# A spectral filter beside a gated MLP: the inverse 32-point product with high and low parts stacked on 128 partitions

## The chip, the cores and the metric

The kernel runs on one core of a Trainium2 chip. The metric is the device time of one execution in microseconds, the median over runs. The program is written with a tile framework: it traces instructions in program order, and a planner with its own cost estimates then orders each engine's instructions and sets all semaphores.

## The reference

```python
def reference(A_x, A_w_r, A_w_i, B_x, B_w_gate, B_w_up, B_w_down):
    xn = _layernorm(A_x, axis=-1)                       # x: 1 x 2048 x 576
    X = rfft2(xn, axes=(-2, -1)) * (A_w_r + 1j * A_w_i) # 2048 x 289 complex weights
    A = irfft2(X, s=(2048, 576))
    g, u = xn @ B_w_gate, xn @ B_w_up                   # 576 -> 4608
    return A_x + A + (sigmoid(g) * u) @ B_w_down        # 4608 -> 576
```

All inputs and the output are fp32.

## The kernel before

Two computations share one core. The gated MLP gives most of the matmuls: 36 slices of the 4608 hidden columns, for each of two halves ("pairs") of the 2048 rows. A slice of one half is a *unit*: seven products of seven matmuls of 512 columns (L710, into the PSUM banks `pA`, `pB`, `pE`), with ScalarE copying banks out (L788 to L806) and VectorE combining them (L803, L823, L825). The products of the down projection are matmuls of 288 columns into `ps` (L1060), taken out by VectorE or ScalarE (L994 is one such addition); a unit's seven turns each carry some of those.

The spectral part runs in pieces between the turns of the second half. Matmuls are fp32r, and a factor is split into a high part (what the format keeps) and a low part (the rest). The transform over the 2048 rows is taken as 64 x 32, over the 576 columns as one matrix; there are `NQ` = 290 columns of frequencies.

- `phase1b` (16 calls): the column transform and the 64-point one, which writes high and low parts to DRAM (`sc1`).
- `phase2` (16 calls): the 32-point transform forward, times the weights (`ri`, here `wr` and `wi`), and the 32-point transform back, into DRAM (`sc2`). In the forward product, the contraction of 64 (real and imaginary parts of 32) is doubled to 128 by having the high parts on the first 64 partitions and the low parts on the other 64; two matrices (`bm[:, 0]`, `bm[:, 1]`) give main sum and correction on two halves of the output, and VectorE adds the halves. In the inverse product two places (of the 64) lie on the 128 partitions, with a matrix that doesn't mix them; high and low parts are two tiles `zh`, `zl`, and three matmuls are accumulated for each pair of places: high by high, low by high, high by low.
- `phase3` (16 calls): the 64-point transform back, and the columns, added to the result.

Each phase is a Python generator. A `yield` ends its share of one schedule step; a schedule step is one turn of a unit (one product), and every active generator is taken on by one share in it, oldest first. When the calls begin stands in one line, start and distance in schedule steps; before the first call of a phase, `stage2` or `stage3` frees the room of the phase before and loads the constant matrices:

```python
U1, U2, U3 = (0, 4.1), (76, 4.1), (151, 4.5)
for (base, rate), phase, n in ((U1, phase1b, NT), (U2, phase2, N2 // 2), (U3, phase3, NT)):
    for t in range(n):
        begin.setdefault(1 + base + int(t * rate), []).append(lambda t=t, phase=phase: phase(t))
```

PSUM tiles from `pair(...)` are two banks; all of them, `pb`, `pc`, `py`, `pz`, `pe` of the phases and `ps` of the down products, come from the same two buffers in turn, so a new pair waits until the one before last has been taken out. A tile with `bufs=1` has one buffer: its next user waits for the last reader. Nearly all loads and stores are issued from the one queue of SyncE (SP), in order; a DMA that waits there holds back the ones behind it, among them the next units' weights (`w` from `wsp`, L323) and the down weights (`wf` from `fsp`, L957).

L1100 are the additions that gather the parts of the down products late in the last stage.

Of the kernel before, what the change touches and what calls it, by code (L numbers as in the profile page):

```python
# [9 lines left out]
F32 = mybir.dt.float32  # L10
F32R = mybir.dt.float32r
I32 = mybir.dt.int32
AF = mybir.ActivationFunctionType
OP = mybir.AluOpType
# [29 lines left out]
KR = 3 * REM  # L44


U1, U2, U3 = (0, 4.1), (76, 4.1), (151, 4.5)


KOF = np.array(list(range(1, HD, 2)) + [0] + list(range(0, HD + 1, 2)))  # L50
# [18 lines left out]
def _cplx(m):  # L69

    return np.block([[m.real, m.imag], [-m.imag, m.real]])


def _constants():
    out = {}

    mid = np.arange(HD) - (D - 1) / 2
    ang = 2 * np.pi * mid[:, None] * KOF[None, :] / D
    t = np.zeros((P, 2, 5, NQ), np.float32)
    for e, v in ((0, np.cos(ang)), (1, -np.sin(ang))):  # L80
        m = np.where(FREQ, v - (v.mean(0) if e == 0 else 0), 0.0)
        hi, lo = _split(m)
        for part, w in ((0, hi), (1, lo)):
            t[:, e, 2 * part] = w[:P]
            t[:, e, 2 * part + 1] = w[P:2 * P]
        t[:KR, e, 4] = np.concatenate([hi[2 * P:], hi[2 * P:], lo[2 * P:]])
    out["cf"] = t.reshape(P, 10 * NQ)


    s1 = np.arange(N1)  # L90
    k1 = np.arange(N1)
    am = np.zeros((P, N2, 2, P), np.float32)
    ai = np.zeros((P, N2, 2, P), np.float32)
    for s2 in range(N2):
        ph = 2 * np.pi * (((N2 * s1[:, None] + s2) * k1[None, :]) % S) / S
        m = _cplx(np.exp(-1j * ph))
        am[:, s2, 0], am[:, s2, 1] = _split(m)
        m = _cplx(np.exp(1j * ph).T)
        ai[:, s2, 0], ai[:, s2, 1] = _split(m)
    out["am"] = am.reshape(P, N2 * 2 * P)  # L100
    out["ai"] = ai.reshape(P, N2 * 2 * P)


    s2 = np.arange(N2)
    ph = 2 * np.pi * ((s2[:, None] * s2[None, :]) % N2) / N2
    bh, bl = (v.reshape(2, N2, N1).transpose(1, 0, 2).reshape(N1, N1) for v in _split(_cplx(np.exp(-1j * ph))))
    none = np.zeros_like(bl)
    bi = _cplx(np.kron(np.exp(1j * ph), np.eye(2)))
    at = np.arange(P).reshape(2, N2, 2)
    bi = bi[at.transpose(2, 0, 1).ravel()][:, at.transpose(1, 0, 2).ravel()]  # L110
    b = np.stack([np.block([[bh, bl], [bh, none]]), np.block([[bl, bh], [none, bh]]), *_split(bi)], 1)
    out["bm"] = b.reshape(P, 4 * P)


    a = np.where((KOF == 0) | (KOF == HD), 1.0, 2.0)[:, None] / (D * S) * FREQ[:, None]
    ang = 2 * np.pi * KOF[:, None] * (QTR[None, :] + 0.5) / D
    t = np.zeros((P, 2, 2, 2, HQ), np.float32)
    r = np.zeros((P, 2, HD), np.float32)
    for e, m in ((0, a * np.cos(ang)), (1, a * np.sin(ang))):
        m[KOF == (HD, 0)[e]] = 0.0  # L120
        hi, lo = _split(m)
        for k, rows in enumerate((slice(0, P), slice(NQ - P, NQ))):
            t[:, e, k, 0], t[:, e, k, 1] = hi[rows], lo[rows]
        h, l = np.zeros((2, FR, HD), np.float32)
        for s, v in ((h, hi), (l, lo)):
            v = v[P:NQ - P]
            o = ODD[P:NQ - P]
            s[o, (1 - e) * HQ:(2 - e) * HQ] = v[o]
            s[~o, e * HQ:(e + 1) * HQ] = v[~o]
        r[:3 * FR, e] = np.concatenate([h, h, l])  # L130
    out["di"] = np.concatenate([t.reshape(P, 8 * HQ), r.reshape(P, 2 * HD)], 1)
    out["id"] = np.eye(P, dtype=np.float32)
    return out
# [6 lines left out]
def _layout(x, w_r, w_i, w_gate, w_up, w_down):  # L140

    ks = np.concatenate([np.arange(KT * P), np.tile(np.arange(KT * P, HD), 4)])
    w = np.stack([w_gate[COLS], w_up[COLS]]).reshape(2, 2, HD, NF, P)[:, :, ks]
    w = w[[1, 1, 0, 0], [0, 1, 1, 0]].reshape(4, KT + 1, P, NF, P).transpose(3, 2, 0, 1, 4)
    v = np.stack([w_r, w_i])[:, :, KOF].reshape(2, N2, 2, N2 // 2, 2, NQ).transpose(3, 2, 1, 0, 4, 5)
    v = np.broadcast_to(v[:, :, None], (N2 // 2, 2, 2, N2, 2, 2, NQ))
    x = x.reshape(S, D)[ROWS][:, COLS]
    xt = x[:, np.argsort(COLS)].reshape(NT, P, 2, HD)
    xt = np.stack([xt[:, :, 0], xt[:, :, 1, ::-1]], 2)
    xt = xt[..., ks].reshape(NT, P, 2, KT + 1, P).transpose(0, 4, 2, 3, 1)  # L150
    xg = x.reshape(NT, P, 2, HD)[TPP:, ..., ks].reshape(2, TPC, P, 2, KT + 1, P).transpose(0, 3, 5, 4, 1, 2).reshape(2, 2, P, (KT + 1) * CW)
    lay = {"x": x.reshape(NT, P, D), "xt": xt.reshape(NT, P, 2 * (KT + 1) * P), "xg": xg, "ri": v.reshape(N2 // 2, P, 4 * NQ),
           "w": w.reshape(NF, P, 4 * (KT + 1) * P), "wd": w_down[:, COLS].reshape(NF, P, D)}
    return {k: np.ascontiguousarray(a) for k, a in lay.items()}
# [9 lines left out]
def spectral_glu_kernel(ctx: ExitStack, tc: tile.TileContext, x, xt, xg, ri, w_in, w_down, out):  # L164
# [3 lines left out]
    def f32(ap):  # L168
        return ap.bitcast(F32)
# [6 lines left out]
    def pair(name):  # L176
        return ps.tile([P, 2, 512], F32, tag="pp", name=name, bufs=2)
# [21 lines left out]

    rowd = tc.dram_tile([2, NT, P], F32, name="rowd")  # L200
    sc1 = tc.dram_tile([2, N2 * P, NQ], F32, name="sc1")
    sc2 = tc.dram_tile([N2 * P, NQ], F32, name="sc2")
    spill = tc.dram_tile([TPP * P, D], F32, name="spill")
    wsp = [tc.dram_tile([P, NX * 5 * P], F32, name=f"wsp{f}") for f in range(NF)]
    wdsp = [tc.dram_tile([P, 2 * D], F32, name=f"wdsp{f}") for f in range(NF)]
# [342 lines left out]

    def phase2(i):
        pool, bm, zz = R["pool"], R["bm"], R["zz"]  # L550
        kl = 2 * i
        x2 = pool.tile([P, 2, 2, NQ], F32R, tag="x2", name=f"x2{i}", bufs=2)
        nc.sync.dma_start(f32(x2), sc1.rearrange("a (q h kl) n -> (a q) h kl n", h=2, kl=N2)[:, :, kl:kl + 2])
        w = pool.tile([P, 2, 2, NQ], F32, tag="ri", name=f"ri{i}", bufs=2)
        nc.sync.dma_start(w.rearrange("p a j n -> p (a j n)"), ri[i])
        wr, wi = w[:, 0], w[:, 1]
        yield
        yield
        yield
        half = slice(0, N1), slice(N1, P)  # L560
        s, c = (pool.tile([P, 2, NQ], F32, tag=f"s{h}", name=f"s{h}{i}") for h in range(2))
        for h, o in enumerate((s, c)):
            yield
            pb = pair(f"pb{i}_{h}")
            for j in range(2):
                nc.tensor.matmul(pb[:, j, :NQ], bm[:, h, :], x2[:, h, j, :], start=True, stop=True)  # L566
            nc.scalar.activation(o, pb[:, :, :NQ], AF.Copy)
        yield
        for h, o in enumerate((s, c)):
            nc.vector.tensor_tensor(s[half[h]], o[half[h]], o[half[1 - h]], op=OP.add)  # L570
        yield
        sw = pool.tile([P, 2, NQ], F32, tag="sw", name=f"sw{i}")
        for k in range(4):
            o, v = (slice(N2 * m, N2 * (m + 1)) for m in (k, k ^ 1))
            nc.scalar.activation(sw[o], s[v], AF.Copy, scale=-1.0 if k % 2 == 0 else 1.0)
        z = pool.tile([P, 2, NQ], F32, tag="z", name=f"z{i}")
        nc.vector.tensor_tensor(z, wr, s, op=OP.mult)
        yield
        nc.vector.tensor_tensor(sw, wi, sw, op=OP.mult)
        nc.vector.tensor_tensor(z, z, sw, op=OP.add)  # L580
        yield
        zh, zl = zz[i % len(zz)]
        nc.scalar.activation(zh, z, AF.Copy)
        yield
        nc.vector.tensor_tensor(zl, z, f32(zh), op=OP.subtract)
        yield
        yield
        pc = pair(f"pc{i}")
        for j in range(2):
            for n, (k, m) in enumerate(((2, zh), (2, zl), (3, zh))):  # L590
                nc.tensor.matmul(pc[:, j, :NQ], bm[:, k, :], m[:, j, :], start=n == 0, stop=n == 2)  # L591
        u = pool.tile([P, 2, NQ], F32, tag="u", name=f"u{i}", bufs=2)
        nc.scalar.activation(u, pc[:, :, :NQ], AF.Copy)  # L593
        nc.sync.dma_start(sc2.rearrange("(p kl) n -> p kl n", kl=N2)[:, kl:kl + 2], u)

    def phase3(t):
        pool, di, dr = R["pool"], R["di"], R["dr"]
        u = pool.tile([P, 2, NQ], F32, tag="u3", name=f"u3{t}", bufs=2)
        nc.sync.dma_start(u, sc2[2 * t * P:(2 * t + 2) * P].rearrange("(j p) n -> p j n", j=2))
        ai = pool.tile([P, 2, 2, P], F32R, tag="ai", name=f"ai{t}", bufs=2)  # L600
        load_r(ai, con["ai"][:, t * 4 * P:(t + 1) * 4 * P].rearrange("p (a h m) -> p a h m", a=2, h=2))
        if t < TPP:
# [3 lines left out]
            a = acc[t]  # L606
        yield
        yield
        yield
        uh = pool.tile([P, 2, NQ], F32R, tag="uh", name=f"uh{t}")  # L610
        ul = pool.tile([P, 2, NQ], F32R, tag="ul", name=f"ul{t}")
# [59 lines left out]
    def stage2():  # L671
        pool = room("2")
        R["bm"] = bm = pool.tile([P, 4, P], F32R, name="bmt")
        load_r(bm, con["bm"].rearrange("p (k m) -> p k m", k=4))
        zh = pool.tile([P, 2, NQ], F32R, name="zh")
        zl = pool.tile([P, 2, NQ], F32R, name="zl")
        R["zz"] = [(zh, zl)]
        yield

    def stage3():  # L680
# [891 lines left out]
```

## Time and profile before

| | |
|---|---|
| median of 3 runs | 1375.08 us (1374.96 to 1375.41) |
| profiled execution | 1374.97 us; its span 1373.2 us |
| busy, of the span | TensorE 1360.3 us, weight loads 1201.3, VectorE 1069.9, ScalarE 776.1 |
| `phase2`'s first load to `phase3`'s first load | 894.8 to 1106.8 us |
| last stage's last inverse product (L619) | 1340.1 us |

"Busy" is the time in which an engine had at least one instruction running. Matmuls overlap in their pipeline, so a matmul's listed duration is longer than what it takes of TensorE's time. In the rows of the profile, a line begins with the source line and the engine; `out<-in` are tiles with their numbers left out. A row of durations has min/median/max in ns. A row of waits reads: who waited, for whom, us in total, times, longest.

### The profile page before, as it was taken

What the parts mean: (1) busy time and instruction counts of PE and PEld (TensorE: products, weight loads), DVE (VectorE), ACT (ScalarE), POOL (GpSimd) and SP (SyncE); (2) the same over time, 40 slices, a digit from 0 to 9 for tenths busy, and PEclk for the clock granted to TensorE, in tenths of its full rate; (3) what the DMA queues carried; (4) which work ended last, traced back from release to release, by engine and by line L of the source; (5) the groups of instructions that cost most, each with busy time, mean ns of one, the idle gap of its engine ahead of it and who ended that gap; (6) DMA issues with size and microseconds to landing.
All of it is one profiled execution on the core that took longest, in us unless ns stands there. A gap on an engine that the chain in (4) does not pass through costs nothing.

```text
span 1373.2 us, 20459 instructions
## 1 busy us (share of the span) xinstructions
PE 1360.3 (99%) x7656; PEld 1201.3 (87%) x7656; DVE 1069.9 (78%) x1555; ACT 776.1 (57%) x1228; POOL 3.3 (0%) x5
## 2 busy tenths in 40 slices
PE   8999999999999999999999999999999999999998
PEld 6888888888888888998888898988888888899887
DVE  7988888787878787999458668667878847777885
ACT  6644767677777767744245545447767634443432
POOL 0000000000000000000000000000000000000000
PEclk9999999999999999999999999999999999999999
DMA  7567786767676766595888878788989787775643
GB/s 258 200 250 284 267 317 251 287 261 267 266 268 260 274 262 256 212 316 179 286 261 269 264 242 251 217 310 304 307 303 314 231 280 254 225 236 174 197 147 87
DMA packets 127058, 346.56 MB, mean 252 GB/s; under 512 B 12816, under 2 KB 34096, under 8 KB 122224
## 3 DMA queue, kind: packets, MB, share of 16 engines
q1 hardware_dynamic: 125968, 343.94, 72.1%
q8 instruction: 61, 1.00, 0.3%
q10 hardware_dynamic: 992, 1.31, 0.3%
q14 instruction: 37, 0.30, 0.1%
HBM read 208.74 MB, written 136.46 MB: 251 GB/s over the span
## 4 chain that ended last, share of the span: by engine, by line
PE 88%; DVE 9%; ACT 2%; issue 1%; DMA 1%; DVEq 0%; ACTq 0%
PE pB L710 23%; PE ps L1060 22%; PE pE L710 15%; PE pA L710 14%; PE po L849 5%; PE pd L527 2%; PE pe L650 1%; PE pc L591 1%; PE py L619 1%; PE pa L543 1%; DVE acc L858 1%; PE pb L566 1%; DVE ys L825 1%; DVE w L284 1%; DVE hs L981 0%
## 5 line engine op out<-in xcount | busy, mean ns | idle before, releaser
L710 PE MATMUL pB<-X,w 128*128 128x512 f32 x1484 | 376.8, 392 | 1.0 <-ACT v L801 0.7
L1060 PE MATMUL ps<-wf,hs 128*128 128x288 f32 x2436 | 360.8, 295 | 1.2 <-DVE ev L655 1.2
L1060 PEld LDWEIGHTS ps<-wf,hs 128*128 128x128 f32 x2436 | 343.4, 188 | 16.4 <-ACT u L593 1.3
L710 PEld LDWEIGHTS pB<-X,w 128*128 128x128 f32 x1484 | 269.5, 188 | 52.5 <-ACT v L801 4.1
L710 PE MATMUL pE<-X,w 128*128 128x512 f32 x1064 | 269.3, 391 | 0.0
L710 PE MATMUL pA<-X,w 128*128 128x512 f32 (+1 forms) x1006 | 253.9, 389 | 0.7 <-ACT X L476 0.2
L710 PEld LDWEIGHTS pE<-X,w 128*128 128x128 f32 x1064 | 194.2, 188 | 35.7 <-DVE ys L803 0.4
L710 PEld LDWEIGHTS pA<-X,w 128*128 128x128 f32 x1006 | 182.3, 188 | 34.6 <-ACT g L798 0.9
L981 DVE TENSOR_TENSOR hs<-ys,hs 128x1024 fp32r<-128x1024 f32 (+1 forms) x105 | 124.7, 1187 | 39.6 <-ACT hs L978 38.5
L282 ACT ACTIVATE w<-raw 128x768 fp32r<-128x768 f32 (+1 forms) x106 | 100.3, 948 | 54.0 <-DVE raw L306 28.7
L978 ACT ACTIVATE hs<-ys 128x1024 fp32r<-128x1024 f32 (+1 forms) x105 | 108.0, 1028 | 24.7 <-PE ps L1060 19.1
L825 DVE TENSOR_TENSOR ys<-ys,g 128x1024 f32<-128x1024 f32 x67 | 81.9, 1223 | 3.7 <-DVE ys L823 0.5
L284 DVE TENSOR_TENSOR w<-raw,w 128x512 fp32r<-128x512 f32 (+1 forms) x106 | 81.7, 771 | 2.5 <-ACT w L282 2.3
L788 ACT ACTIVATE pB<-pA 128x512 f32<-128x512 f32 x68 | 39.6, 582 | 73.9 <-PE pA L710 71.6
L806 ACT ACTIVATE g<-pB 128x512 f32<-128x512 f32 x68 | 40.6, 597 | 65.2 <-PE pB L710 65.0
L803 DVE TENSOR_TENSOR ys<-v,pE 128x512 f32<-128x512 f32 x68 | 46.5, 684 | 39.1 <-ACT v L801 38.5
L974 DVE TENSOR_TENSOR ys<-ys 128x1024 f32<-128x1024 f32 (+1 forms) x60 | 71.1, 1185 | 0.6
L849 PEld LDWEIGHTS po<-wb,hp 128*128 128x128 f32 x468 | 65.0, 188 | 2.8 <-ACT hp L887 0.4
L849 PE MATMUL po<-wb,hp 128*128 128x288 f32 x468 | 67.1, 296 | 0.0
L795 ACT ACTIVATE v<-pB 128x512 f32<-128x512 f32 x68 | 40.5, 595 | 45.7 <-PE pB L710 45.3
L801 ACT ACTIVATE v<-pB 128x512 f32<-128x512 f32 x68 | 40.5, 596 | 40.8 <-PE pB L710 40.1
L823 DVE TENSOR_TENSOR ys<-v,pE 128x512 f32<-128x512 f32 x67 | 45.8, 684 | 22.2 <-PE pE L710 21.6
(185 smaller groups left out, 1583.2 us busy)
## 6 DMA issues: line engine op xcount, KB each, us to landing
w<-wsp SPq DMA_DIRECT2D x246, 320.0 KB, 3.9
wsp<-w SPq DMA_DIRECT2D x34, 2240.0 KB, 7.2
wf<-fsp SPq DMA_DIRECT2D x105, 288.0 KB, 4.3
fsp<-wf SPq DMA_DIRECT2D x98, 288.0 KB, 3.3
raw<-in_w SPq DMA_DIRECT2D x34, 768.0 KB, 6.6
x<-sc SPq DMA_DIRECT2D x16, 580.0 KB, 5.2
ri<-in_ri SPq DMA_DIRECT2D x16, 580.0 KB, 5.7
dt<-in_wd SPq DMA_DIRECT2D x32, 288.0 KB, 5.7
```

Source lines behind the costliest of these rows:

```text
L282: placed(nc.scalar.activation(o[:, :, :3, :], src, AF.Copy))
L284: placed(nc.vector.tensor_tensor(o[:, :, 3:, :], src[:, :, :KT, :], f32(o[:, :, :KT, :]), op=OP.subtract))
L710: strictly(nc.tensor.matmul(bank[:, cols], w[:, sw, :], X[:, x, sx, cols], start=start and j == 0, stop=stop and j == len(steps) - 1, skip ...
L803: nc.vector.tensor_tensor(y1, v[:, 1], bank["E"], op=OP.add)
L806: nc.scalar.activation(g[:, 1], bank["B"], AF.Sigmoid)
L823: nc.vector.tensor_tensor(place(u, 0), v[:, 0], bank["E"], op=OP.add)
L825: nc.vector.tensor_tensor(h, h, g, op=OP.mult)
L849: nc.tensor.matmul(pd[b], l, r, start=start, stop=stop)
L974: nc.vector.tensor_tensor(o, at(a), at(b), op=op)
L978: nc.scalar.activation(hs[:, :, 0], o, AF.Copy)
L981: nc.vector.tensor_tensor(hs[:, :, 1], o, f32(hs[:, :, 0]), op=OP.subtract)
L1060: nc.tensor.matmul(pd[:, s], h[:, g, a, m], w[:, g, b], start=q == 0 and not seeded, stop=q == len(parts_) - 1, skip_group_check=seeded)
```

## The change

The inverse product gets the form that the forward one has. Two places of `z` (128 partitions: place 0 on the first 64, place 1 on the rest) are split so that the high part of a place stays on its 64 partitions and its low part goes to the other 64, in a tile `zz[:, h]` for each place `h`. Two matrices (`bm[:, 2]`, `bm[:, 3]`) with the high and low parts of the transform give the main sum (high and low by high) on the first 64 partitions of the output and the correction (high by low) on the other 64, in one matmul for each place and `j`. The result leaves in two tiles `u`, and `sc2` holds main sum and correction apart, twice the size; `phase3` loads both and adds them. The places are dealt to the steps four in a row instead of two and two; the layout of `ri` on the host follows. `ri` has one buffer instead of two and is asked for later; `z` has two instead of one; some yields and the start of `phase3` move.

```diff
-U1, U2, U3 = (0, 4.1), (76, 4.1), (151, 4.5)
+U1, U2, U3 = (0, 4.1), (76, 4.1), (153, 4.3)
...
+    ih, il = (v.reshape(N1, 2, N2).transpose(0, 2, 1).reshape(N1, N1) for v in _split(_cplx(np.exp(1j * ph))))
     none = np.zeros_like(bl)
-    bi = _cplx(np.kron(np.exp(1j * ph), np.eye(2)))
-    at = np.arange(P).reshape(2, N2, 2)
-    bi = bi[at.transpose(2, 0, 1).ravel()][:, at.transpose(1, 0, 2).ravel()]
-    b = np.stack([np.block([[bh, bl], [bh, none]]), np.block([[bl, bh], [none, bh]]), *_split(bi)], 1)
+    b = np.stack([np.block(v) for v in ([[bh, bl], [bh, none]], [[bl, bh], [none, bh]], [[ih, il], [ih, none]], [[ih, none], [ih, il]])], 1)
...
-    sc2 = tc.dram_tile([N2 * P, NQ], F32, name="sc2")
+    sc2 = tc.dram_tile([2, N2 * P, NQ], F32, name="sc2")
...
     def phase2(i):
         pool, bm, zz = R["pool"], R["bm"], R["zz"]
-        kl = 2 * i
-        x2 = pool.tile([P, 2, 2, NQ], F32R, tag="x2", name=f"x2{i}", bufs=2)
-        nc.sync.dma_start(f32(x2), sc1.rearrange("a (q h kl) n -> (a q) h kl n", h=2, kl=N2)[:, :, kl:kl + 2])
-        w = pool.tile([P, 2, 2, NQ], F32, tag="ri", name=f"ri{i}", bufs=2)
-        nc.sync.dma_start(w.rearrange("p a j n -> p (a j n)"), ri[i])
-        wr, wi = w[:, 0], w[:, 1]
-        yield
+        x2 = pool.tile([P, 4, NQ], F32R, tag="x2", name=f"x2{i}", bufs=2)
+        nc.sync.dma_start(f32(x2), sc1.rearrange("a (q k) n -> (a q) k n", k=N1)[:, 4 * i:4 * i + 4])
         yield
         yield
...
             pb = pair(f"pb{i}_{h}")
             for j in range(2):
-                nc.tensor.matmul(pb[:, j, :NQ], bm[:, h, :], x2[:, h, j, :], start=True, stop=True)
+                nc.tensor.matmul(pb[:, j, :NQ], bm[:, h, :], x2[:, 2 * j + h, :], start=True, stop=True)
             nc.scalar.activation(o, pb[:, :, :NQ], AF.Copy)
+            if h == 0:
+                w = pool.tile([P, 2, 2, NQ], F32, tag="ri", name=f"ri{i}", bufs=1)
+                nc.sync.dma_start(w.rearrange("p a j n -> p (a j n)"), ri[i])
+                wr, wi = w[:, 0], w[:, 1]
...
-        z = pool.tile([P, 2, NQ], F32, tag="z", name=f"z{i}")
+        z = pool.tile([P, 2, NQ], F32, tag="z", name=f"z{i}", bufs=2)
         nc.vector.tensor_tensor(z, wr, s, op=OP.mult)
         yield
         nc.vector.tensor_tensor(sw, wi, sw, op=OP.mult)
         nc.vector.tensor_tensor(z, z, sw, op=OP.add)
         yield
-        zh, zl = zz[i % len(zz)]
-        nc.scalar.activation(zh, z, AF.Copy)
-        yield
-        nc.vector.tensor_tensor(zl, z, f32(zh), op=OP.subtract)
-        yield
-        yield
-        pc = pair(f"pc{i}")
+        yield
+        yield
+        for h in range(2):
+            nc.scalar.activation(zz[half[h], h], z[half[h]], AF.Copy)
+        yield
+        for h in range(2):
+            nc.vector.tensor_tensor(zz[half[1 - h], h], z[half[h]], f32(zz[half[h], h]), op=OP.subtract)
+        yield
         for j in range(2):
-            for n, (k, m) in enumerate(((2, zh), (2, zl), (3, zh))):
-                nc.tensor.matmul(pc[:, j, :NQ], bm[:, k, :], m[:, j, :], start=n == 0, stop=n == 2)
-        u = pool.tile([P, 2, NQ], F32, tag="u", name=f"u{i}", bufs=2)
-        nc.scalar.activation(u, pc[:, :, :NQ], AF.Copy)
-        nc.sync.dma_start(sc2.rearrange("(p kl) n -> p kl n", kl=N2)[:, kl:kl + 2], u)
+            yield
+            pc = pair(f"pc{i}_{j}")
+            for h in range(2):
+                nc.tensor.matmul(pc[:, h, :NQ], bm[:, 2 + h, :], zz[:, h, j, :], start=True, stop=True)
+            u = pool.tile([P, 2, NQ], F32, tag="u", name=f"u{i}_{j}", bufs=2)
+            nc.scalar.activation(u, pc[:, :, :NQ], AF.Copy)
+            nc.sync.dma_start(sc2.rearrange("a (q k) n -> (a q) k n", k=N1)[:, 4 * i + 2 * j:4 * i + 2 * j + 2], u)

     def phase3(t):
         u = pool.tile([P, 2, NQ], F32, tag="u3", name=f"u3{t}", bufs=2)
-        nc.sync.dma_start(u, sc2[2 * t * P:(2 * t + 2) * P].rearrange("(j p) n -> p j n", j=2))
+        v = pool.tile([P, 2, NQ], F32, tag="v3", name=f"v3{t}")
+        for a, o in enumerate((u, v)):
+            nc.sync.dma_start(o, sc2[a, 2 * t * P:(2 * t + 2) * P].rearrange("(j p) n -> p j n", j=2))
...
         yield
         yield
+        yield
+        nc.vector.tensor_tensor(u, u, v, op=OP.add)
         yield
         uh = pool.tile([P, 2, NQ], F32R, tag="uh", name=f"uh{t}")
...
     def stage2():
-        zh = pool.tile([P, 2, NQ], F32R, name="zh")
-        zl = pool.tile([P, 2, NQ], F32R, name="zl")
-        R["zz"] = [(zh, zl)]
+        R["zz"] = pool.tile([P, 2, 2, NQ], F32R, name="zz")
```

More of the change, by code (lines that the diff above doesn't have):

```diff
@@ L144, in _layout @@
     w = w[[1, 1, 0, 0], [0, 1, 1, 0]].reshape(4, KT + 1, P, NF, P).transpose(3, 2, 0, 1, 4)
-    v = np.stack([w_r, w_i])[:, :, KOF].reshape(2, N2, 2, N2 // 2, 2, NQ).transpose(3, 2, 1, 0, 4, 5)
+    v = np.stack([w_r, w_i])[:, :, KOF].reshape(2, N2, N2 // 2, 2, 2, NQ).transpose(2, 4, 1, 0, 3, 5)
     v = np.broadcast_to(v[:, :, None], (N2 // 2, 2, 2, N2, 2, 2, NQ))
```

## Prediction

> **What bounds the kernel now.** I read the page's engine rows first, then the chain that ended last, then busy time in stretches.
>
> ```profile
> span 1373.2 us, 20459 instructions
> PE 1360.3 (99%) x7656; PEld 1201.3 (87%) x7656; DVE 1069.9 (78%) x1555; ACT 776.1 (57%) x1228; POOL 3.3 (0%) x5
> PE 88%; DVE 9%; ACT 2%; issue 1%; DMA 1%; DVEq 0%; ACTq 0%
> ```
>
> TensorE is busy in 1360.3 of 1373.2 us, and 88% of the chain is TensorE's. So TensorE time that goes away is worth its full length, unless TensorE then waits for something. The changed stages are the middle one (`phase2`, 895 to 1106 us) and the last (`phase3`, 1106 to 1340 us); the limits there are read from stretches (columns: PE, PEld, DVE, ACT, POOL busy, clock, DMA share, GB/s):
>
> ```profile
> 100.00:400.00 300.00, 299.77 (x1611) 262.36 (x1610) 250.50 (x362) 200.43 (x294) 0.00 (x0) 1.00 0.72 274
> 895.00:1106.00 211.00, 210.44 (x1180) 186.53 (x1179) 162.06 (x201) 135.60 (x204) 0.00 (x0) 1.00 0.86 292
> 1106.00:1280.00 174.00, 173.68 (x1052) 155.88 (x1051) 123.76 (x186) 72.81 (x135) 0.00 (x0) 1.00 0.72 232
> 1280.00:1340.00 60.00, 59.09 (x364) 53.18 (x363) 51.92 (x80) 24.27 (x50) 0.00 (x0) 1.00 0.55 170
> 980.00:990.00 10.00, 10.00 (x56) 8.69 (x56) 9.53 (x12) 8.07 (x13) 0.00 (x0) 1.00 0.90 310
> 990.00:1000.00 10.00, 10.00 (x58) 9.00 (x58) 9.77 (x14) 6.58 (x10) 0.00 (x0) 1.00 0.91 314
> 1060.00:1070.00 10.00, 10.00 (x60) 9.01 (x59) 9.73 (x13) 7.58 (x13) 0.00 (x0) 1.00 0.87 294
> 1300.00:1310.00 10.00, 9.09 (x54) 7.86 (x53) 9.93 (x14) 3.38 (x7) 0.00 (x0) 1.00 0.66 202
> ```
>
> TensorE idles 0.56 us in the middle stage and 0.32 + 0.91 = 1.23 us in the last. VectorE is at 162.06/211 = 77% and (123.76 + 51.92)/234 = 75%; slices of 95 to 98% (980 to 1000, 1060) leave TensorE full, and the one at 99% (1300) doesn't. So VectorE is the engine that TensorE waits for first. The clock is 1.00 throughout.
>
> **What goes.** Per step of `phase2` the inverse product had six matmuls (L591: two places by three products) and will have four: 96 become 64 in 16 steps. A matmul's listed 295 ns is its latency; what it costs is the distance to the next:
>
> ```profile
> L591 PE MATMUL pc<-zh,bmt x64: 291/295/307, 931.4 to 1101.9; 128*128 128x290 f32 x64
> 926.34 0.43 PE L566 MATMUL pb<-x,bmt 128*128 128x290 f32 x2
> ...
> 926.61 1.75 PE L710 MATMUL pA<-X,w 128*128 128x512 f32 x7
> ...
> 931.37 0.29 PE L591 MATMUL pc<-zh,bmt 128*128 128x290 f32 x1
> 931.50 0.30 PE L591 MATMUL pc<-zl,bmt 128*128 128x290 f32 x1
> 931.64 0.43 PE L591 MATMUL pc<-zh,bmt 128*128 128x290 f32 x2
> 931.90 0.30 PE L591 MATMUL pc<-zl,bmt 128*128 128x290 f32 x1
> 932.04 0.29 PE L591 MATMUL pc<-zh,bmt 128*128 128x290 f32 x1
> ```
>
> From 931.37 to 932.04 are five distances: 0.134 us each. A group of only two (the forward product L566, 926.34 to 926.61) takes 0.27 us, so cutting the product into two groups of two adds nothing. 32 x 0.134 = 4.29 us go. Here the Trainium skill (TensorE: Matmul & The Clock Gate, Back-to-back issue gap) gives columns / 2.4 GHz + 2.5 ns, 123 ns for 290 columns; by that 3.95 us would go. The row says 134 ns and decides.
>
> **What comes, off TensorE.** The nearest rows:
>
> ```profile
> L583 ACT ACTIVATE zh<-z x16: 672/690/694, 924.1 to 1092.4; 128x580 fp32r<-128x580 f32 x16
> L593 ACT ACTIVATE u<-pc x16: 654/657/661, 932.4 to 1102.2; 128x580 f32<-128x580 f32 x16
> L585 DVE TENSOR_TENSOR zl<-z,zh x16: 755/764/764, 925.0 to 1093.1; 128x580 fp32r<-128x580 f32 x16
> L570 DVE TENSOR_TENSOR s<-s x32: 755/757/760, 914.3 to 1083.2; 64x580 f32<-64x580 f32 x32
> L575 ACT ACTIVATE sw<-s x64: 683/687/691, 915.0 to 1085.2; 32x580 f32<-32x580 f32 x64
> L613 DVE TENSOR_TENSOR ul<-u,uh x16: 751/754/765, 1113.1 to 1336.2; 128x580 fp32r<-128x580 f32 x16
> ```
>
> - The high part: one copy on 128 partitions becomes two on 64. Fewer partitions save nothing (687 ns on 32, 690 on 128), so ScalarE gets 16 x 0.69 = 11.0 us. The product leaves PSUM in two copies: 16 x 0.657 = 10.5 us. ScalarE goes from 135.6 to 157.1 us, 64% to 76% of the stage's 206.7 us.
> - The low part: two subtractions on 64 partitions for one (757 ns against 764), 16 x 0.757 = 12.1 us more VectorE in the middle stage: 162.1 to 174.2 us, 84%.
> - Last stage: main sum plus correction, 16 more additions, nearest row 0.754 us: 12.1 us, VectorE from 175.7 to 187.8 of 234 us, 80%. This work is hidden where VectorE has room; where it has none, TensorE waits for the whole 0.75 us.
> - One more yield ahead of `uh` and a start three steps later but at rate 4.3 for 4.5: the last item then starts one step earlier (218 for 219) and splits at the same step, so the tail keeps its place. Nothing on the path.
>
> What TensorE pays of this: the middle stage has a model in 100 to 400 us, where VectorE at 83.5% and ScalarE at 67% cost 0.23 us in 300. Ends: 0 us (the slices at 95 to 98% cost nothing) and 1.3 us (each slice pushed over full by the 0.69 us that it gets more in 10 us passes the excess on: 0.22 at 980, 0.46 at 990, 0.42 at 1060, 0.2 in two others). ScalarE's part can show in the wait for a bank's copy (below). I take 0.6. Last stage:
>
> ```profile
> 1300.94 4.14 DVE L1100 TENSOR_TENSOR qs<-qs 128x1152 f32<-128x1152 f32 x3
> 1304.99 1.11 DVE L655 TENSOR_TENSOR ev<-pe,od 128x432 f32<-128x432 f32 x2
> 1306.25 1.03 PE L1060 MATMUL ps<-wf,hs 128*128 128x288 f32 x6 [0.91 <-DVE ev L655]
> PE ps L1060 <- DVE ev L655: 1.2, 2, 0.9
> ```
>
> VectorE's three gathering additions (4.14 us) hold `ev` back, and TensorE waits 0.91 us for the pair of banks that `ev` frees. One new addition falls into this jam: +0.75 us. Ends: -0.9 (the order moves and the jam is gone) and +1.5 (two additions in it). I take 0.7.
>
> **PSUM pairs.** A step takes four pairs (two forward, two inverse) for three, from the same two buffers. The second forward group of a step and the inverse group now fall on different steps of the schedule (offsets 3, 4, 13, 14, four apart: one pair in each step), where before the inverse one (12) met a forward one (4). Cost 0, in that ScalarE empties a pair in 0.657 us and a schedule step is 11.04 / 4.1 = 2.7 us.
>
> **Transfers.** More: 16 writes of 290 KB in the middle stage, 16 reads of as much in the last. `x2` reads the same bytes in half as many runs.
>
> ```profile
> w<-wsp SPq DMA_DIRECT2D x78, 320.0 KB, 4.1
> sc<-u SPq DMA_DIRECT2D x16, 290.0 KB, 3.6
> u<-sc SPq DMA_DIRECT2D x16, 290.0 KB, 3.4
> SPq L594 <- ACT u L593: 24.4, 16, 2.2
> ```
>
> 16 x 0.297 MB in 207 us is 23 GB/s on 292: share 0.86 to about 0.93. SP's queue stands at each write until the copy is done (24.4 us in 16), and this doubles; behind it stand the loads of `w`. 78 of those in 211 us, seven to a unit, make a unit 18.9 us, and a slice is loaded a unit ahead for 4.1 us to landing: cover 14 us. Cost 0; without that cover each late slice would cost TensorE its lateness. Into the last stage: both reads wait for the last write as one did; the extra yield (2.7 us) covers the second read's landing (3.4 us, issued 0.4 us later) and the addition, 0.
>
> **The weights `ri`** have one buffer for two and are asked for after the first forward copy:
>
> ```profile
> L577 DVE TENSOR_TENSOR z<-ri,s x16: 754/758/765, 919.0 to 1084.6; 128x580 f32<-128x580 f32 x16
> L579 DVE TENSOR_TENSOR sw<-ri,sw x16: 751/756/764, 921.5 to 1086.0; 128x580 f32<-128x580 f32 x16
> DMA to landing us min/median/max: 4.9/5.7/7.2
> ```
>
> The buffer is free when L579 of one step ends and needed at L577 of the next. Steps are (1084.6 - 919.0)/15 = 11.04 us apart, L579 follows L577 by 1.4 to 2.5, so the gap is 11.04 - 1.9 - 0.76 = 8.4 us for a landing of 5.7 (at most 7.2). Cost 0 at 2.7 us of slack; ends 0 and, if each came late, the rival below. The request itself now stands on SP for L579, ahead of `w`; covered as above.
>
> **Sum.** -4.29 + 0.6 + 0.7 = -3.0 us. The profiled execution took 1374.97 us (1373.2 of span and 1.8 around it), 0.1 below the median of 1375.08: 1372.0 for it, **1372.1** as a median.
>
> **The rivals.**
> - *Spent in VectorE and ScalarE waits, no change measured.* Both jams pass on in full: 1.3 us in the middle stage, 1.5 us in the last, and the wait of a product for its bank doubles:
>
> ```profile
> PEld pB L710 <- ACT v L801: 0.8, 1, 0.8
> PE pB L710 <- ACT v L801: 0.6, 1, 0.6
> ```
>
>   (TensorE's own part is 0.6; as much again.) For it: VectorE and ScalarE lose room at once. Against: 20 us at 97% VectorE without a wait. 1374.97 - 4.29 + 1.3 + 1.5 + 0.6 = 1374.1.
> - *Slower: `ri` comes late.* With the transfers at 0.93 its landing stretches past the 8.4 us; L577 stands on VectorE, and behind it the additions that free `ps` pairs and `pE`. TensorE has about a schedule step (2.7 us) of cover, so waits begin to cost at a landing of 8.4 + 2.7 = 11.1 us, 16 us for each us past that: at 11.3 nothing of the gain is left, and at 11.6 it is 8 us more than my forecast, 1380. For it: transfers at 0.9 already. Against: the longest landing was 7.2. The Trainium skill (DMA: Bandwidth & Descriptors, Where 436 GB/s comes from) puts a core's share of HBM at about 358 GB/s, above the 315 that I expect; no run here shows that limit.
> - *More than the sum.* The new order also loses the jam at 1305 and the 0.56 us of the middle stage: 1374.97 - 4.29 - 1.4 = 1369.3. For it: the additions move. Against: VectorE only gets more.
>
> **How the numbers follow.** What a measurement can tell from no change is 0.2%, 2.75 us: 1372.3 to 1377.8. My forecast (1370.5 to 1373): 0.48; spent in waits (to 1376): 0.27; slower: 0.14; more than the sum: 0.11. The forecast's upper part is over the bound, so faster is 0.35 + 0.11 = 0.46, same 0.13 + 0.26 = 0.39, slower 0.15. For 8 in 10 the range leaves out the far end of the slow case and a little below: 1369.3 to 1377.5; the forecast's own is 1370.5 to 1373.
>
> **What would show it.** L591's successor has 64 matmuls at 0.134 us and TensorE's busy time falls by 4.3 us to about 1356; idle time between 895 and 1340 us goes from 1.8 to about 3; VectorE there is some 24 us busier; DMA share in the middle is about 0.93. Wrong it would be if VectorE waits for a transfer of `ri`, if waits for `v`'s copies (L801) grow beyond 1.5 us, or if TensorE idles before the first group of the last stage.

## The result, and the profile after

The changed kernel took 1381.24 us as a median of 6 runs (1378.89 to 1381.53), the kernel before 1375.35 beside it (1374.96 to 1375.98): ratio 1.004, 95% interval 1.0027 to 1.0053. It is 5.9 us slower where the prediction had it 3.0 us faster; measured once more it was 1380.34. (One execution of `v_two_buffers` below took 1905 us and one of `two_buffers_and_pool` 3522; they count in the medians given, which would be 0.1 us lower without them, and not in the ratios.) The profiled execution took 1381.49 us, 1379.7 of it span. The page's first rows and the chain that ended last:

```profile
span 1379.7 us, 20510 instructions
PE 1359.8 (99%) x7624; PEld 1197.8 (87%) x7624; DVE 1092.2 (79%) x1587; ACT 794.9 (58%) x1260; POOL 3.3 (0%) x5
PE 86%; DVE 7%; DMA 3%; ACT 3%; issue 1%; SPq 0%; DVEq 0%; ACTq 0%
```

TensorE has the 32 matmuls fewer (7624 for 7656), but is busy only 0.5 us less, and the rest of the span grew from 12.9 to 19.9 us: 7.0 - 0.5 = 6.5, the whole difference of the spans. DMA and ScalarE now hold 3% of the chain each. By stretches (columns as before):

```profile
100.00:400.00 300.00, 299.78 (x1612) 262.39 (x1611) 250.38 (x362) 200.19 (x293) 0.00 (x0) 1.00 0.72 274
895.00:1106.00 211.00, 206.62 (x1138) 181.34 (x1137) 175.12 (x216) 153.43 (x234) 0.00 (x0) 1.00 0.91 311
1106.00:1280.00 174.00, 170.24 (x1024) 151.52 (x1023) 126.40 (x191) 70.72 (x131) 0.00 (x0) 1.00 0.78 254
1280.00:1340.00 60.00, 59.06 (x362) 53.14 (x362) 52.07 (x81) 26.23 (x54) 0.00 (x0) 1.00 0.62 194
```

The first stage is as it was. In the middle one TensorE idles 4.38 us (0.56 before), in 1106 to 1280 3.76 (0.32), in 1280 to 1340 0.94 (0.91). So half of the loss is in the middle stage and half early in the last. TensorE's waits, first of 895 to 1106 and then of 1106 to 1350 (line waiting, releaser: us in total, times, longest):

```profile
PE pb L559 <- DMA x<-sc: 1.9, 2, 1.0
PE pB L712 <- ACT v L803: 1.7, 3, 0.6
PE ps L1062 <- ACT u L593: 0.6, 2, 0.4
```

```profile
PE pz L639 <- DMA w<-wsp: 1.8, 1, 1.8
PE pe L654 <- DVE z3l L241: 1.6, 1, 1.6
PE ps L1062 <- DVE ev L659: 0.9, 1, 0.9
```

Only `ev` was there before at that length. The two new waits of the last stage start on VectorE, whose own waits say where they come from (the third row is of the middle stage):

```profile
DVE u L612 <- DMA u<-sc: 8.7, 6, 3.7
DVE u L612 <- DMA v<-sc: 6.4, 2, 5.2
DVE z L574 <- DMA ri<-in_ri: 1.1, 1, 1.1
```

The new addition L612 stands up to 5.2 us for its second operand, the correction `v`, which has one buffer for `u`'s two. The timeline shows one such wait and what it does (start, duration, engine, line):

```profile
1142.38 0.76 DVE L612 TENSOR_TENSOR u<-u,v 128x580 f32<-128x580 f32 x1
1145.73 0.39 SPq L601 DMA_DIRECT2D v<-sc  x1
1151.62 0.76 DVE L612 TENSOR_TENSOR u<-u,v 128x580 f32<-128x580 f32 x1 [5.20 <-DMA v<-sc]
1159.30 0.23 DVE L241 TENSOR_TENSOR rp<-py,rp 128x68 fp32r<-128x68 f32 x1
1159.57 0.23 ACT L630 ACTIVATE rp<-py 128x68 fp32r<-128x68 f32 x1 [3.75 <-DVE rp L241]
1159.84 0.20 PEld L639 LDWEIGHTS pz<-idr,rp 128*102 128x102 f32 x2 [2.24 <-ACT rp L630]
1159.85 0.34 PE L639 MATMUL pz<-idr,rp 128*102 128x128 f32 x2 [1.80 <-DMA w<-wsp]
```

The load of the next `v` can't be issued before the addition at 1142.38 has read the last one; SP comes to it at 1145.73, 2.6 us after the buffer is free, it lands some 6 us later, and VectorE stands for 5.20 us. What piles up behind is still there at 1159.30: `rp` comes late, ScalarE has stood 3.75 us for it, and TensorE 1.80. (That last wait is put down to a transfer of `w`; the weight load PEld of the same matmul names ScalarE's `rp`, and the rows above it agree with that.)

The second new wait comes from a stand for `u`, which has two buffers. `z3l` is VectorE's next work after that addition, and TensorE waits for it:

```profile
1189.85 0.77 DVE L612 TENSOR_TENSOR u<-u,v 128x580 f32<-128x580 f32 x1 [3.66 <-DMA u<-sc]
1191.27 0.33 PE L654 MATMUL pe<-dit,z3l 128*128 128x144 f32 x1 [1.65 <-DVE z3l L241]
```

In the middle stage, first the input `x2` of the forward product, then a chain from VectorE to TensorE:

```profile
1026.04 0.32 SPq L594 DMA_DIRECT2D sc<-u  x1
1026.41 0.42 SPq L550 DMA_DIRECT2D x<-sc  x1
...
1033.07 0.51 PE L559 MATMUL pb<-x,bmt 128*128 128x290 f32 x2 [0.97 <-DMA x<-sc]
...
1046.35 0.76 DVE L567 TENSOR_TENSOR s<-s 64x580 f32<-64x580 f32 x1
1047.14 1.39 ACT L572 ACTIVATE sw<-s 32x580 f32<-32x580 f32 x2 [1.06 <-DVE s L567]
1048.55 0.60 ACT L803 ACTIVATE v<-pB 128x512 f32<-128x512 f32 x1
1049.20 1.19 PE L712 MATMUL pB<-X,w 128*128 128x512 f32 x4 [0.61 <-ACT v L803]
```

SP stood at the write of `u` (L594) until 1026.04 and issued `x2` right behind it, 6.7 us ahead of its matmul, where a load of `x2` takes 6.3 us to land (the median; 4.1 to 7.8). Over the 16 items (issues and first matmuls of the timeline) `x2` was asked for 17 to 21 us ahead before; now it is so for seven, and 5.4 to 10.7 us ahead from the eighth on. In the second part VectorE's `s` comes late, ScalarE stands 1.06 us for it, and its next work, the copy of `v` out of `pB`'s bank, is 0.61 us too late for TensorE.

SP's waits in 890 to 1345 have this row:

```profile
SPq L594 <- ACT u L593: 58.6, 30, 5.1
```

### The profile page after: what moved, and what is told of

It reads as the page before. It is cut to its first block, busy times and chain, and to the rows that moved or that the text cites. A ratio compares the mean times of both kernels' runs of the same rounds, so it can differ in the third digit from the quotient of the medians.

```text
span 1379.7 us, 20510 instructions
## 1 busy us (share of the span) xinstructions
PE 1359.8 (99%) x7624; PEld 1197.8 (87%) x7624; DVE 1092.2 (79%) x1587; ACT 794.9 (58%) x1260; POOL 3.3 (0%) x5
## 4 chain that ended last, share of the span: by engine, by line
PE 86%; DVE 7%; DMA 3%; ACT 3%; issue 1%; SPq 0%; DVEq 0%; ACTq 0%
PE pB L712 22%; PE ps L1062 21%; PE pE L712 15%; PE pA L712 14%; PE po L851 5%; PE pd L525 2%; PE pe L654 1%; PE py L623 1%; PE pa L541 1%; ACT sw L572 1%; DMA w<-wsp 1%; DMA x<-sc 1%; DVE acc L860 1%; DVE ys L827 1%; PE b L1138 0%
## 5 line engine op out<-in xcount | busy, mean ns | idle before, releaser
L827 DVE TENSOR_TENSOR ys<-ys,g 128x1024 f32<-128x1024 f32 x67 | 82.0, 1223 | 3.4 <-DVE ys L825 0.5
```

The source lines that it names most:

```text
L827: nc.vector.tensor_tensor(h, h, g, op=OP.mult)
```

## The experiments

The theory after the result had three parts: (A) `v`'s single buffer lets VectorE stand for its transfer; (B) SP's queue, standing at twice as many writes, issues `x2` late; (C) the added operations of VectorE and ScalarE in the middle stage pass small delays on. The rival (D): the matmuls removed were never worth 4.3 us. Each ratio is to the kernel before on the same chip, with its 95% interval; each kernel is the changed one with the edit shown, where nothing else is said.

**v_two_buffers.**

```diff
-        v = pool.tile([P, 2, NQ], F32, tag="v3", name=f"v3{t}")
+        v = pool.tile([P, 2, NQ], F32, tag="v3", name=f"v3{t}", bufs=2)
-        ai = pool.tile([P, 2, 2, P], F32R, tag="ai", name=f"ai{t}", bufs=2)
+        ai = pool.tile([P, 2, 2, P], F32R, tag="ai", name=f"ai{t}", bufs=1)
```

> The changed kernel with two buffers for v3 and, for the room, one for ai. Three theories for what the change lost (TensorE does 4.3 us less and the kernel is 6 us longer, so some 10 us of waits came in). LOADS: in the last stage v has one buffer, its load is asked for only after the addition before, the addition then stands on VectorE for it (15 us of VectorE waits for u and v in the trace), and TensorE waits behind (2.0 us before pz, 1.8 before pe, 0.7 before py): this run about 1377, and VectorE's waits for u and v near 0. QUEUE: SP stands at the 32 writes of u until ScalarE has copied (58.6 us for 24.4), and the loads behind come late, in both stages: about 1380, the waits for u and v smaller. WORK: the added VectorE and ScalarE work itself: no change, 1381.

1377.35 us, 1.0011 (1.0002 to 1.0021): most of the loss is gone. `ai` gave up a buffer because the stage had no room for both, so that had to be measured alone.

**ai_one_buffer, and all three on one chip: changed_again, ai_again, v_again.** The second line of that edit alone, twice; the changed kernel and the whole edit once more.

> The changed kernel with one buffer for ai and v3 still with one: what the room for the second buffer of v3 cost or brought by itself. If the second buffer of v3 took the 3.9 us off: 1381 to 1382 here. If the move of ai's loads did: 1377.5.

> The changed kernel unaltered, timed beside the two below: 1381 if the first timing holds; 1379.5 if its place there was the chip's.

> The changed kernel with one buffer for ai. If the single buffer of v3 is the cause: as changed_again within 0.7. If the order in which ai is loaded is: 2 us below it.

> The changed kernel with one buffer for ai and two for v3: 1377.4. The distance to ai_again is what the second buffer of v3 is worth: 2 to 4 us by the theory LOADS (TensorE's wait before pz, 1.8 us, and before pe go with it), 0 if it was all ai.

`ai_one_buffer` 1379.31, 1.0032 (1.002 to 1.0043). On one chip: changed 1380.34, 1.0036 (1.0024 to 1.0049); with `ai` at one buffer 1379.81, 1.0027 (1.0016 to 1.0038); with `v` at two besides 1377.03, 1.0011 (1.0002 to 1.002). `ai` is worth at most half a microsecond, which these runs don't tell from nothing; `v`'s second buffer is worth 2.8 us (2.0 by the first pair, `ai_one_buffer` against `v_two_buffers`, on two chips). Waits in 1106 to 1350 with one buffer of `v` (ai_again), then with two (v_again):

```profile
PE pz L639 <- ACT rp L630: 1.8, 1, 1.8
...
DVE u L612 <- DMA v<-sc: 6.1, 2, 5.4
```

```profile
PE ps L1062 <- DVE ev L659: 0.9, 1, 0.9
PE pz L639 <- DMA ai<-c_ai: 0.2, 1, 0.2
...
DVE u L612 <- DMA u<-sc: 9.3, 8, 2.8
DVE u L612 <- DMA v<-sc: 0.5, 1, 0.5
```

VectorE's stand for `v` falls from 6.1 to 0.5 us, and TensorE's 1.8 for `rp` goes with it. It still stands 9.3 us for `u`, 2.8 us at most at a time, and no TensorE wait follows from that; in the changed kernel one did from the stand of 3.66 us. So it is the length of a single stand that costs, not the sum. (A) is shown for the stand of 5 us; the wait behind `u` was gone with `ai` at one buffer already.

**no_correction_in_last.**

```diff
-        for a, o in enumerate((u, v)):
+        for a, o in enumerate((u,)):
-        nc.vector.tensor_tensor(u, u, v, op=OP.add)
```

> The changed kernel with the last stage's part left out: the correction is written but neither loaded nor added, so the output lacks it. LOADS: all waits of the last stage go, 1376.5. WORK: 12 us of VectorE go from the last stage, 1377 to 1379. QUEUE: the stage's queue has one load less in each call, about 1380. Against the run with two buffers it gives the price of the addition by itself.

1376.15 us, 1.0003 (0.9994 to 1.0012). 1.2 us below `v_two_buffers` beside it: about the price of the addition and the second read, once nothing waits for `v`, though the two intervals overlap.

**writes_on_pool_queue, two_buffers_and_pool.** The first is the edit shown, the second that and the two lines of `v_two_buffers`.

```diff
-            nc.sync.dma_start(sc2...[:, 4 * i + 2 * j:4 * i + 2 * j + 2], u)
+            nc.gpsimd.dma_start(sc2...[:, 4 * i + 2 * j:4 * i + 2 * j + 2], u)
```

> The changed kernel with the 32 writes to sc2 issued by POOL and not SP. QUEUE: SP stands no more for u, x2 is asked for some 20 us ahead as in the kernel before, TensorE's two waits for x2 (1.1 us each) and part of the last stage's go: 1376 to 1378. LOADS and WORK: 1380 to 1382; LOADS has v's wait unchanged.

> Two buffers for v3 (one for ai) and the writes to sc2 from POOL, together. Two buffers alone took 3.9 us off the changed kernel and POOL's writes 0.9. If LOADS and QUEUE are two causes: 1376.4, no wait of TensorE for x2. If POOL's writes gain nothing without their cause (only WORK is left): 1377.4, as with two buffers alone.

1380.36, 1.0034 (1.0021 to 1.0047), and 1376.77, 1.0008 (0.9998 to 1.0017). `x2` is asked for 16.6 to 22.5 us ahead in all 16 items again, and its waits are gone from TensorE's list (890 to 1345, writes_on_pool_queue):

```profile
PE pB L712 <- ACT v L803: 2.1, 3, 1.1
PE pz L639 <- DMA w<-wsp: 1.7, 1, 1.7
```

But the time hardly moves: 0 to 0.9 us below the changed kernel's two medians, 0.3 to 0.6 below `v_two_buffers`. Of the 1.9 us of waiting for `x2`, 0.4 came back as waiting for ScalarE (1.7 us before, 2.1 now). TensorE started the product behind the stand for `rp` at 1158.28 us, 1.57 us ahead of the changed kernel (1159.85). Then the clock that TensorE was granted fell: to 0.73 in the next stretch of 5 us, and twelve matmuls took 2.52 us for 1.85 (two rows of this run, then one of the changed kernel):

```profile
1160.00:1165.00 5.00, 5.00 (x26) 4.49 (x25) 1.17 (x2) 1.97 (x4) 0.00 (x0) 0.73 0.69 229
1158.45 2.52 PE L1062 MATMUL ps<-wf,hs 128*128 128x288 f32 x12
```

```profile
1160.02 1.85 PE L1062 MATMUL ps<-wf,hs 128*128 128x288 f32 x12
```

At 1163.8 both kernels start the same product, and the lead is gone. The queue is late as (B) says; what that costs isn't shown, since the clock falls in one of these two profiles and not in the other.

**one_split_op, all_three, one_copy_two_subs, two_copies_one_sub.** These take the added half-height operations back: one copy, one subtraction, or both on 128 partitions. `one_split_op` does it in the changed kernel, the others in `two_buffers_and_pool`; `all_three` has both edits. Where only one of them is taken back, all high parts go to `zz[:, 0]` and all low parts to `zz[:, 1]`.

```diff
-        for h in range(2):
-            nc.scalar.activation(zz[half[h], h], z[half[h]], AF.Copy)
+        nc.scalar.activation(zz[:, 0], z, AF.Copy)
...
-        for h in range(2):
-            nc.vector.tensor_tensor(zz[half[1 - h], h], z[half[h]], f32(zz[half[h], h]), op=OP.subtract)
+        nc.vector.tensor_tensor(zz[:, 1], z, f32(zz[:, 0]), op=OP.subtract)
```

> The changed kernel with one high-part copy and one subtraction on 128 partitions for the two and two on 64, as the kernel before has them; the two tiles of zz then hold high and low parts where the matrices expect them stacked, so the output is another. 11 us less ScalarE and 12 us less VectorE in the middle stage. WORK: the waits of a product for a bank's copy and of ps for u's copy (3.1 us in all) go: 1377 to 1378. QUEUE: a little, since u's copies come earlier: 1380. LOADS: 1381.

> The same with one high-part copy and one subtraction on 128 partitions for the two and two on 64 (the output is another, since zz does not hold what the matrices expect). If the three causes add up (3.9 + 0.9 + 2.8 us off 1381.2): 1373.6, and only the added copies of u and the additions in the last stage keep it from the 1371.0 that 4.3 us less TensorE would give. If there is a fourth cause that none of these touches: 1375 or more.

> two_buffers_and_pool (1376.8) with one high-part copy on 128 partitions for two on 64, and the two subtractions kept: 11 us of ScalarE go from the middle stage, VectorE's work stays (the output is another, since zz does not hold what the matrices expect). With both reduced it was 1373.5, 3.3 us less. If ScalarE is what TensorE waits for, as the waits for the copies of u and v say: 1373.5 to 1374.5. If VectorE: 1376 to 1377.

> The other half: two high-part copies, one subtraction on 128 partitions; 12 us of VectorE go from the middle stage, ScalarE's work stays (the output is another). ScalarE: 1376 to 1377. VectorE: 1373.5 to 1374.5.

`one_split_op` 1378.47, 1.0019 (1.0009 to 1.0029), 1.9 to 2.8 us below the changed kernel's two medians, but with executions from 1374.6 to 1381.6. Beside `two_buffers_and_pool` (1376.77): one copy 1375.67, 1.0002 (0.9993 to 1.0011), 1.1 us less; one subtraction 1373.94, 0.9989 (0.998 to 0.9998), 2.8 less; both 1373.48, 0.9985 (0.9976 to 0.9994), 3.3 less. (The two with one operation ran on another chip; the kernel before took 1375.57 there and 1375.50 here.) TensorE's waits for `v`'s copy in 895 to 1106 with one copy and two subtractions, then with two copies and one subtraction:

```profile
PE pB L711 <- ACT v L802: 2.0, 3, 1.0
```

```profile
PE pB L711 <- ACT v L802: 0.4, 1, 0.4
```

Both rows name ScalarE; taking work from ScalarE leaves the wait, taking it from VectorE removes most of it. ScalarE is only the link, as at 1046. (C) is shown, and VectorE's 16 subtractions are the larger part of it.

**before_two_products.** The kernel before, without the third product: 32 matmuls fewer and nothing else.

```diff
-            for n, (k, m) in enumerate(((2, zh), (2, zl), (3, zh))):
-                nc.tensor.matmul(..., start=n == 0, stop=n == 2)
+            for n, (k, m) in enumerate(((2, zh), (2, zl))):
+                nc.tensor.matmul(..., start=n == 0, stop=n == 1)
```

> The kernel before with the third product (high by low) of the inverse left out and nothing else: 32 matmuls of 290 columns fewer, no other engine's work changed; the output lacks that correction. If TensorE's time is worth its full length here: 1375.5 - 4.3 = 1371.2. If something else sets the pace in the middle stage, it stays near 1375.

1372.86 us, 0.9982 (0.9973 to 0.9991): 2.6 us, with 1.2 to 3.7 by the interval. The prediction's 4.29 lies outside, so (D) holds in part. Busy time of TensorE fell by 2.1 us to 1358.2. The middle stage:

```profile
895.00:1106.00 211.00, 210.22 (x1159) 184.46 (x1159) 163.79 (x202) 135.68 (x205) 0.00 (x0) 1.00 0.88 295
```

The idle column hardly moves, 0.56 to 0.78 us. The starts of the matmuls say more. Take each at the usual distance to the next for its shape, the median in the kernel before (227 ns at 512 columns, 132 at 288, 133 at 290): then all matmuls add up to 1341.3 us before and 1337.0 here, 4.3 less. What the distances have beyond that rises by 2.2 us, and 1.7 of it lies between 895 and 1106 (3.2 us before, 4.9 here). So the matmuls were worth their 4.3 us, and the same stage gave 1.7 back in short waits; 0.7 of these lie before products into `ps`, whose weight loads waited longer in all for `u`'s copy (before, then here):

```profile
PEld ps L1060 <- ACT u L593: 1.3, 6, 0.2
```

```profile
PEld ps L1060 <- ACT u L593: 1.9, 5, 0.6
```

**middle_stretched.** `two_buffers_and_pool` with the middle stage at a slower rate.

```diff
-U1, U2, U3 = (0, 4.1), (76, 4.1), (153, 4.3)
+U1, U2, U3 = (0, 4.1), (76, 4.3), (156, 4.1)
```

> two_buffers_and_pool with the starts (76, 4.3) and (156, 4.1) for the second and third phase: the middle stage gets three steps more, the last stage three less, its end stays. ScalarE in the middle falls from 73% to some 70%, VectorE in the last stage rises from 79% to 81%. If ScalarE's lack of room in the middle is the rest of the cost: 1 us less, 1375.8, near the kernel before; if VectorE in the last stage is as short: 1377 to 1378.

1379.74, 1.0036 (1.0023 to 1.0049): 3 us more, above what either case expected. The stretches of `two_buffers_and_pool`, then of this kernel:

```profile
895.00:1106.00 211.00, 208.00 (x1147) 182.84 (x1147) 175.59 (x217) 154.05 (x235) 16.97 (x31) 1.00 0.92 312
1106.00:1280.00 174.00, 173.97 (x1051) 156.15 (x1050) 129.68 (x196) 73.77 (x135) 0.54 (x1) 1.00 0.81 259
```

```profile
895.00:1106.00 211.00, 208.99 (x1149) 182.65 (x1148) 175.54 (x217) 153.06 (x234) 16.43 (x30) 1.00 0.91 311
1106.00:1280.00 174.00, 171.30 (x1031) 152.92 (x1030) 129.13 (x193) 71.66 (x133) 1.08 (x2) 1.00 0.81 258
```

TensorE idles 2.0 us in the middle for 3.0, but 2.7 us behind it for 0.03: the last stage, started later and run faster, loses more than the middle one gains.

**swap_on_pool, low_on_pool.** Work taken from ScalarE and from VectorE to GpSimd, both in `two_buffers_and_pool`.

```diff
-            nc.scalar.activation(sw[o], s[v], AF.Copy, scale=-1.0 if k % 2 == 0 else 1.0)
+            nc.gpsimd.tensor_scalar(sw[o], s[v], -1.0 if k % 2 == 0 else 1.0, None, op0=OP.mult)
```

```diff
-            nc.vector.tensor_tensor(zz[half[1 - h], h], z[half[h]], f32(zz[half[h], h]), op=OP.subtract)
+            (nc.vector, nc.gpsimd)[h].tensor_tensor(zz[half[1 - h], h], z[half[h]], f32(zz[half[h], h]), op=OP.subtract)
```

> As two_buffers_and_pool, and the four copies of sw (0.69 us each, 44 us of ScalarE in the middle stage) done by POOL. WORK says that ScalarE's lack of room is what is left: ScalarE in the middle falls from 154 to 110 us, the waits for u's and v's copies go, 1373 to 1374, below the kernel before. Against it: POOL's copies may take longer than 0.7 us and z waits for them, or slow VectorE's own instructions: 1377 or more.

> two_buffers_and_pool (1376.8) with the low part of one place in two subtracted on POOL: VectorE has 12 us less in the middle stage, as in two_copies_one_sub (1373.9), and the output is unchanged. If VectorE's time is the cause and POOL keeps up: 1374 to 1375.5, below the kernel before. POOL's copies of 32 partitions took 1.8 us in swap_on_pool and VectorE's instructions beside them 17% longer; if that decides, 1377 to 1382.

1430.3, 1.0401 (1.0384 to 1.0419), and 1378.54, 1.0023 (1.0014 to 1.0032): both worse than 1376.77. The first kernel's group of swaps (count, busy us, mean ns, then what ended GpSimd's idle time), and VectorE's wait for them in 890 to 1345:

```profile
L572 POOL TENSOR_SCALAR sw<-s 32x580 f32<-32x580 f32 x64 | 116.5, 1820 | 999.4 <-DMA wf<-fsp 910.0 <-DVE s L567 86.4
```

```profile
DVE sw L576 <- POOL sw L572: 59.2, 16, 5.0
```

A swap takes 1820 ns for ScalarE's 687, and each item has four of them ahead of VectorE's product with `sw`: VectorE stands 59.2 us for them. The mean granted clock of this execution is 0.988, so by estimate some 17 of its 1427.5 us of span are the clock's. In the second kernel it is the two engines in each other's way (duration ns min/median/max):

```profile
L585 DVE TENSOR_TENSOR zz<-z,zz x16: 755/756/2210, 919.5 to 1100.3; 64x580 fp32r<-64x580 f32 x16
L585 POOL TENSOR_TENSOR zz<-z,zz x16: 1435/1446/2153, 920.2 to 1101.8; 64x580 fp32r<-64x580 f32 x16
```

TensorE's wait for `v` is down to 0.4 us there, but 1.3 us for `ys` (VectorE) have come, and the wait for `u` (ScalarE) is 1.6 for 0.8. So no version that does all of the work was faster than the kernel before; the nearest is `two_buffers_and_pool`, whose interval holds 1.

## Why the prediction was wrong

The chain of runs, each beside the last: changed 1380.3 (1381.2 in its first runs); `ai` and `v` 1377.0; writes on the other queue 1376.8; the half-height operations 1373.5; and 1372.9 with the third product alone removed from the kernel before. So 2.6 us were to be had, and some 7.5 were paid (on two chips, where the kernel before took 1375.7 and 1375.5): 2.8 for `v`'s buffer, 3.3 for the split into halves, 0.3 and 0.5 for queue and `ai` (neither told from nothing), 0.6 left over, in which the second copy of `u`, the addition and the added transfers would lie. The parts need not add outside this order. Counted by the distances of matmuls, the 6.5 us between the two profiles are 4.3 less for the matmuls and 10.8 more beyond the usual distances, 5.8 in the middle stage and 4.7 in 1106 to 1280. Idle time of 895 to 1340 was to go from 1.8 to about 3 us, and went to 9.1.

*Failed: "covers the second read's landing ... and the addition, 0".* The largest single error. I priced the landing of one item's two reads against the yield, not the wait of the next item's read for the buffer of this one, though I had worked out exactly that for `ri`. `v` has one buffer: its load is issued after the addition, stands behind what SP has (2.6 us at 1143), and lands in some 6 us; of the 9.2 us from one addition to the next there VectorE stood for 5.2. My cost of 0 was 2.8 us (2.0 by the other pair).

*Failed: the middle stage's 0.6, ends 0 and 1.3.* It measured 3.3 us. I took VectorE's load against each 10-us slice and passed on the overflow alone. What the runs show in its place: a delay of VectorE goes through ScalarE into a bank that TensorE needs (1046 to 1049), and the 16 added subtractions account for 2.8 of the 3.3 us. Why slices of 97% were harmless before isn't shown. It isn't ScalarE's room alone, since one copy less in each item left 2.0 us of that wait. The rival "spent in waits" had the mechanism, at 1374.1; its size, 1.3 and 0.6 us in the middle stage, was too small.

*Mis-sized: -4.29.* The distances are as read, and two groups of two cost nothing more. A place in the middle stage after:

```profile
1014.41 0.43 PE L591 MATMUL pc<-zz,bmt 128*128 128x290 f32 x2
1014.68 1.54 PE L712 MATMUL pA<-X,w 128*128 128x512 f32 x6
```

The product has 64 matmuls (median 293 ns listed), and two take 0.27 us. But the same 32 removed by themselves gave 2.6 us, not 4.3: "worth its full length, unless TensorE then waits for something" was said in the first part and its second half was not priced; it was 1.7 us of short waits in the same stage.

*Half right: SP's queue at 0.* I said that its standing would double, and it went from 24.4 us in 16 to 58.6 in 30. I looked for the load behind it only in `w`, for which no product of the middle stage waits; `x2`, the other load there, lost 10 us of its 18. The time hardly moves when this is mended, but the clock fell in that profile; with two buffers of `v`, where it didn't, the other queue brought 0.3 to 0.6 us, not told from nothing. So the 0 is not refuted, and not for the reason that I gave.

*Near in number, not in mechanism: the last stage's 0.7.* It was to come from one more addition in the jam at `ev`. The wait for `ev` stayed at 0.9 us, and the addition measured 1.2 us with its read, once `v` has its buffers. That the numbers are close is luck.

*Small: PSUM pairs at 0.* `pc` is nowhere in the lists of TensorE's waits above, but `ps`, which takes its pairs from the same two buffers, waits 0.6 us for the copy of `u`, and had no such wait of TensorE before.

*Right: `ri`.* VectorE stood once, 1.1 us, and the landing stayed at 5.7 (at most 6.7), so the slower rival's mechanism didn't happen, though its sign did. The second sign came too: waits for `v`'s copies of 1.7 us, over the 1.5 named, and behind these stood what did cost time. VectorE rose by 22.3 us over the whole span (24 said), the DMA share in the middle to 0.91 (0.93), and TensorE had no wait ahead of the last stage's first group worth 0.3 us. Busy time of TensorE was to fall to 1356, and fell to 1359.8: 4.3 us went, and 3.8 us of short waits count as busy. A slip without effect: the last stage's start moved by two steps (151 to 153), not three.

Open: which waits the 1.0 us are that the distances show beside those before `ps`, and what the late queue costs by itself. The changed kernel's executions lie 1378 to 1383 us apart, those before within 1.7 us, and the granted clock has a part in that: in the changed kernel, `writes_on_pool_queue`, `ai_one_buffer` and `ai_again`, with one buffer of `v`, 10 of 30 executions have a mean clock of 0.998 or less; in `v_two_buffers`, `v_again` and `two_buffers_and_pool`, with two, none of the 29 that the ratios use. Five of the ten are the changed kernel's; they took 1381.1 to 1383.2 us, its other six 1378.3 to 1381.5. What makes the clock fall isn't shown: the changed kernel's own profile has the same stand at 1159 and no fall.

## What to carry to other kernels

For every tile that a change adds, write down its buffers, who frees one, when the queue comes to the next load, and the landing: one buffer for two turned a hidden 290 KB read into a 5-us stand of VectorE and 2 to 2.8 us of time. Check this for each load behind a queue that now stands longer, not for the most frequent one alone. And a wait that names an engine tells only the last link: ScalarE's name stood on the waits here, and taking work from VectorE is what removed most of them. Idle time is not all that waits cost either: add up the distances between matmuls beyond the usual ones.

## What the runs showed of the hardware

GpSimd and VectorE can stop each other for a whole instruction. In `low_on_pool` one subtraction of VectorE, begun 0.13 us before one of GpSimd's, took 2210 ns for 756, which is 1454 more, one GpSimd subtraction (1446). One of GpSimd's took 2153, which is 707 more; it began 0.4 us into a VectorE product of 1.23 us (L827). The Trainium skill (SBUF — State Buffer, Who interferes with whom) calls the port that they share an exclusive lock: a VectorE instruction with two inputs in SBUF and a GpSimd one that reads SBUF block each other for the whole instruction. The rows agree. VectorE's additions with one input in PSUM (`qs<-qs,ps`, L996) took their usual 0.75 us beside GpSimd, at 1009.88 for one.

The granted clock can fall for a few us in the middle of a kernel, and a matmul then takes longer: in `writes_on_pool_queue` it reads 0.50 from 1160 to 1162 us and 1.00 again from 1163, right after TensorE had stood 1.71 us, and the group above took 2.52 us for 1.85. By estimate from these rows that cost 1.3 us (0.67 in this group, 0.63 in the three matmuls behind it).

The transfers had more room than I gave them. The rival on `ri` set 358 GB/s beside it as a core's share (the Trainium skill, DMA: Bandwidth & Descriptors, Where 436 GB/s comes from), and one stretch of the changed kernel went past that:

```profile
1120.00:1130.00 10.00, 10.00 (x56) 8.76 (x55) 5.61 (x8) 2.97 (x6) 0.00 (x0) 1.00 1.04 380
```

On one core 380 GB/s passed without TensorE idling, so that figure didn't bind here.
